# Products of zeros in spare PSUM banks, from the balancing to the first up matmuls

## The chip, the cores and the metric

The kernel runs on one core of one Trainium2 chip. The metric is the device time of one execution in microseconds (us); lower is better. A core has five engines that work side by side: PE (TensorE, matrix products), DVE (VectorE), ACT (ScalarE), POOL (GpSimd) and SP (SyncE, which here only issues transfers). Each takes its own instructions in order, and semaphores tie them together.

## The reference

Two parts follow each other. First an attention with sorted blocks: a small matrix of 8 x 8 per batch and head is balanced five times (rows and columns in turn), then it mixes the eight blocks of keys and values, and each block of queries attends to its mixed block. Then a feed-forward part with g = h cos(h).

```python
for _ in range(5):
    P = np.exp(P - np.max(P, axis=-1, keepdims=True))
    P = P / (np.sum(P, axis=-1, keepdims=True) + 1e-09)
    P = P / (np.sum(P, axis=-2, keepdims=True) + 1e-09)
k_sorted = np.einsum('bhij,bhjcd->bhicd', P, k_b)
v_sorted = np.einsum('bhij,bhjcd->bhicd', P, v_b)
scores = scale * np.matmul(q_b, k_sb.transpose(0, 1, 2, 4, 3))
attn = softmax(scores)
x = np.matmul(attn, v_sb)            # 3072 tokens x 512
h = x @ w_in                         # 512 -> 2048
out = (h * np.cos(h)) @ w_out        # 2048 -> 512
```

Batch 4, heads 8, sequence 768 (8 blocks of 96), head size 64.

## The kernel before, in words

The 3072 tokens are worked in eight chunks n of four blocks u each. For a chunk the stages are: scores (`qk`: products L422 or L427, row maximum L482 and subtraction L488 on DVE), exponent (`expo`, ACT, L506), transposition of the weights (`p_transpose`: eight transposes L532, and a copy to `pT`), weights times values (`av`, products L545, reciprocal L552 and scaling L554 on DVE), transposition of the result (`x_transpose`, L572, and a copy to `xT`), then `up` (products L585, cosine on ACT L589, product with h on DVE L592) and `down` (L609). The order of all of this is written out by hand from L674 on; no scheduler moves anything. Copies out of PSUM go through `copy_on`, so all of them on ACT have the line L288 and all on DVE L290.

Ahead of that stands the balancing (L266 to L352), for two groups g of two batches. Each of the four further rounds `it` has, per group, an exponent on ACT (L331), a product that sums (`product`, L262, tile `sk`) and three small steps on DVE (reciprocal L350, and L323 and L326 in `balance`). Between the rounds stand the transposes of the first queries (`q_products`, L301), whose results ACT copies to `q_turned` (twice, from two tiles `q_ps`). At the end of the last round DVE writes the balanced matrix spread out for the products, `bd` (L282).

Then come the sorted keys: `k_sort_0` makes products of key columns with `bd` (L360, tile `ks`) and copies them to `kTs` in four pieces. It is called for key columns 0 to 15 (copies on DVE), 32 to 39 (DVE), 16 to 31 (ACT) and 40 to 47 (ACT). `v_turn` (L436) makes `bdv`, and `v_sort_b` (L450, tile `vs`) makes eight columns of sorted values at a time and copies them to `vS` on ACT. The first calls of `qk` and the first up matmuls follow.

PSUM has eight banks here, in two pools. `acc` has two buffers of one bank, `big` three buffers of two banks (1024 float32 per partition). A tile in `big` always takes a buffer of two banks, also where it fills one or less: the tiles of `q_products`, `v_turn`, `p_transpose`, and those of `k_sort_0` and `v_sort_b` when they are told to use `big` (`*B` in the order; `*C` is `acc`).

`keep_warm(times)` (L216) takes a new tile `idle` in `big` and multiplies a matrix of zeros, `warm`, by one of its columns repeated 512 times, so many times (L220). Nothing reads the result. It is called with 17 ahead of the balancing, with 2 behind the first pair of `product`, and with 3 in the first further round.

Of the kernel before, what the change touches and what calls it, by code (L numbers as in the profile page):

```python
# [10 lines left out]
FP32 = mybir.dt.float32  # L11
BF16 = mybir.dt.bfloat16
# [6 lines left out]
def kernel(  # L19
# [15 lines left out]
    nc = tc.nc  # L35
    B, H, S, D = q.shape
    nb = sort_net.shape[-1]
    blk = S // nb
# [6 lines left out]
    H2 = H // 2  # L45
    NG = B // 2
    NN = 2 * H2 * nb
    IC = 4
# [5 lines left out]
    NB = H2 * nb  # L54

    const = ctx.enter_context(tc.tile_pool(name="const", bufs=1))
# [35 lines left out]
    def load(buf, r, src):  # L92
        nc.gpsimd.dma_start(out=buf[r:r + 64], in_=src)
# [7 lines left out]
    QR, NQ = 4, 3  # L101
# [101 lines left out]

    ones(0)
    order = const.tile([blk, blk], BF16, name="order")
    half_pi = const.tile([128, 1], FP32, name="half_pi")
    nc.vector.memset(half_pi[:], math.pi / 2)
    warm = const.tile([128, 128], BF16, name="warm")
    nc.vector.memset(warm[:], 0.0)
    nc.vector.memset(vperm[:, CD:], 0.0)  # L210
    nc.vector.memset(kbuf[:64, :32 * D], 0.0)

    early = const.tile([128, 1], FP32, name="early")
    nc.scalar.activation(early[:], half_pi[:], AF.Exp)

    def keep_warm(times):  # L216

        idle = big.tile([128, 512], FP32, name="idle", tag="big")
        for _ in range(times):
            nc.tensor.matmul(  # L220
                idle[:], warm[:], warm[:, :1].to_broadcast([128, 512]), start=True, stop=True)

    keep_warm(17)


# [34 lines left out]
    def product(lhs, rhs):  # L260
        ps = acc.tile([128, nb], FP32, name="sk", tag="acc")
        nc.tensor.matmul(  # L262
            ps[:], lhs.rearrange("p x j -> p (x j)"), rhs, start=True, stop=True)
        return ps

    for g in range(NG):  # L266
        nc.vector.reciprocal(ci[g][:], cs[g][:])
        nc.vector.scalar_tensor_tensor(
            L[g][:], rows_of, ci[g][:], along(E[g]), op0=ALU.mult, op1=ALU.mult)
    sk = [product(L[g], maskj[:]) for g in range(NG)]  # L270
    keep_warm(2)
# [22 lines left out]
    q_ps = {}  # L294

    def q_products(n, z, lo, hi, pool, tag):
        if lo == 0:
            q_ps[n, z] = pool.tile([128, 2, IC, QR, blk // QR], BF16, name="qps", tag=tag)
        for i in range(lo, hi):
            e, hp, r = i // (2 * QR), i // QR % 2, i % QR  # L300
            nc.tensor.transpose(  # L301
                q_ps[n, z][hp * D:(hp + 1) * D, e, :, r],
                q_rows[:, (z * 2 + e) * 2 + hp, r * D:(r + 1) * D], ident[:blk, :blk])
# [25 lines left out]
    for it in range(4):  # L329
        for g in range(NG):  # L330
            nc.scalar.activation(E[g], T[g], AF.Exp, scale=ci[g][:])  # L331
        if it == 3:
            copy_on(A, *turned[0])
        sk = [product(same, E[g]) for g in range(NG)]
        if it == 1:
            q_products(0, 0, 0, 12, big, "big")
        elif it == 2:
            turned = q_turn(0, 0, big, "big", 12)
            q_products(0, 1, 0, 8, big, "big")
        elif it == 3:  # L340
            turned = q_turn(0, 1, big, "big", 8)
            copy_on(A, *turned[0])
        keep_warm(3 if it == 0 else 0)
        if it == 1:

            nc.gpsimd.tensor_copy(held[:], cs[1][:])
            for z in range(3):
                load_w_in(z)
        for g in range(NG):
            nc.vector.reciprocal(rr[g], sk[g][:])  # L350
            if it < 3 or g == 0:
                balance(g)  # L352
# [4 lines left out]
    MH = H2 * IC  # L357
# [4 lines left out]

    def k_sort_0(t0, nt, eng, pool, tag):

        ps = pool.tile([128, nt, 2 * MH], FP32, name="ks", tag=tag)
        for t in range(nt):
            k_products(ps, t, t0 + t, slice(64, 128),
                       bds[0][64:, H:, :IC])
        ms, ts = slice(0, MH), slice(t0, t0 + nt)
        psv = ps.rearrange("p t (e m) -> p e m t", e=2)  # L370
        for hp in range(2):
            for x in range(2):
                copy_on(eng, kT[0][hp * D:(hp + 1) * D, hp + x, ms, ts],
                        psv[x * D:(x + 1) * D, hp])

    def k_cross(t0, nt, eng, pool, tag):

        ps = pool.tile([128, nt, 2 * MH], FP32, name="ks", tag=tag)
        for t in range(nt):
            k_products(ps, t, t0 + t, slice(64, 128), bds[0][64:, H:, IC:])  # L380
        ms, ts = slice(MH, 2 * MH), slice(t0, t0 + nt)
        copy_on(eng, kT[0][:, ::2, ms, ts], ps.rearrange("p t (e m) -> p e m t", e=2))
        nc.gpsimd.tensor_copy(kT[0][:D, 1, ms, ts], kT[0][D:, 0, ms, ts])
        nc.gpsimd.tensor_copy(kT[0][D:, 1, ms, ts], kT[0][:D, 2, ms, ts])

    def k_sort_1(t0, eng, pool, tag):
        ps = pool.tile([128, 8, 2 * NB], FP32, name="ks", tag=tag)
# [43 lines left out]
    bdv = const.tile([128, 2 * H, nb], BF16, name="bdv")  # L431

    def v_turn(eng=A):
        ps = big.tile([128, 128], FP32, name="bdp", tag="big")
# [7 lines left out]
        return vperm[:, d * blk:d * blk + 128] if permuted else vv[:, d]  # L442

    def v_sort_b(b, d0, nd, eng, pool, tag):
        ps = pool.tile([128, nd, 2 * NB], FP32, name="vs", tag=tag)


        rows, xs = slice(0, 64 + b * 64), slice((1 - b) * H, (2 - b) * H)
        for t in range(nd):
            nc.tensor.matmul(  # L450
                ps[:, t], v_cols(d0 + t, b == 1 or d0 + t >= D // 2)[rows],
                bdv[rows, xs].rearrange("p x i -> p (x i)"), start=True, stop=True)
# [48 lines left out]
    def expo(n, u, on_pe=False):  # L501
        p = p_bufs[cnt[0] % NP]
        cnt[0] += 1


        nc.scalar.activation(  # L506
            p[:, :, :blk], s_t.pop((n, u)).rearrange("p e h c -> p (e h) c"), AF.Exp,
            scale=scale)
# [18 lines left out]

    def p_transpose(n, u, eng, pool, tag):
        p = pb.pop((n, u))
        ps = pool.tile([128, 2 * H2, 128], BF16, name="pps", tag=tag)  # L530
# [147 lines left out]
    load_w_out(2)  # L678
    load_w_out(3)
    k_sort_0(0, 16, V, *C)  # L680
    v_turn()
    k_sort_0(32, 8, V, *B)
    k_sort_0(16, 16, A, *C)
    k_sort_0(40, 8, A, *C)
    v_sort_b(0, 0, 8, A, *C)
    qk(0, 0)
    qk(0, 1)
    v_sort_b(0, 8, 8, A, *B)
    v_sort_b(0, 16, 8, A, *C)
    expo(0, 0, True)  # L690
    v_sort_b(0, 24, 8, A, *C)
    load(kbuf, 0, kin_d[1])
    qk(0, 2)
    v_sort_b(0, 40, 8, A, *C)
    p_transpose(0, 0, A, *B)
    v_sort_b(0, 56, 8, A, *C)
    expo(0, 1, True)
    qk(0, 3)
    v_sort_b(0, 48, 8, A, *C)
    v_sort_b(0, 32, 8, A, *C)  # L700
    p_transpose(0, 1, A, *B)
# [12 lines left out]
    up(0, 0, 0, 2 * blk)  # L714
    p_transpose(0, 2, A, *C)
    up(0, 1, 0, 2 * blk)
# [227 lines left out]
```

## Time and profile before

| | us |
|---|---|
| three timed runs | 244.58, 245.59, 245.89; median 245.59 |
| the profiled execution | 245.65 |
| its span, first to last instruction | 243.9 |
| PE busy | 233.2 (96% of the span) |
| DVE busy | 173.8 (71%) |
| ACT busy | 157.6 (65%) |
| POOL busy | 88.0 (36%) |

The profile is one execution on the chip. A row of the timeline gives start and duration in us from the start of the span, the engine (PE are the products, PEld the loading of their fixed operand), the line of the kernel, the operation, the tile written and the tiles read, the shape, and how often. In brackets stands the engine's idle time before it and what ended it. The granted clock is the share of TensorE's full clock, 1.00 or 0.50 here. All products of zeros together have this row (busy time; mean ns of one):

```profile
L220 PE MATMUL idle<-warm 128*128 128x512 bf16 x22 | 7.0, 474 | 1.0 <-DVE warm L209 1.0
```

### The profile page before, as it was taken

What the parts mean: (1) busy time and instruction counts of PE and PEld (TensorE: products, weight loads), DVE (VectorE), ACT (ScalarE), POOL (GpSimd) and SP (SyncE); (2) the same over time, 40 slices, a digit from 0 to 9 for tenths busy, and PEclk for the clock granted to TensorE, in tenths of its full rate; (3) what the DMA queues carried; (4) which work ended last, traced back from release to release, by engine and by line L of the source; (5) the groups of instructions that cost most, each with busy time, mean ns of one, the idle gap of its engine ahead of it and who ended that gap; (6) DMA issues with size and microseconds to landing.
All of it is one profiled execution on the core that took longest, in us unless ns stands there. A gap on an engine that the chain in (4) does not pass through costs nothing.

```text
span 243.9 us, 5384 instructions
## 1 busy us (share of the span) xinstructions
PE 233.2 (96%) x2172; PEld 148.4 (61%) x2172; DVE 173.8 (71%) x320; ACT 157.6 (65%) x226; POOL 88.0 (36%) x110
## 2 busy tenths in 40 slices
PE   8879899899999999999999999999999999999994
PEld 3569698756576566655666656655565556456553
DVE  5568848996478965887668986898789768625700
ACT  3368866568288984888668956684567366737611
POOL 6359963599771099710443500800000000000000
PEclk9955569999999999999999999999999999999999
DMA  4999999991999961999898959924592660171012
GB/s 49 232 194 170 185 205 232 190 202 57 143 143 144 172 150 55 94 143 212 149 101 139 71 132 157 193 33 105 116 201 59 90 188 0 41 144 43 1 46 86
DMA packets 66681, 30.90 MB, mean 127 GB/s; under 512 B 55392, under 2 KB 62176, under 8 KB 66400
## 3 DMA queue, kind: packets, MB, share of 16 engines
q0 software_dynamic: 24048, 13.64, 41.9%
q1 hardware_dynamic: 42096, 16.72, 31.7%
q8 instruction: 17, 0.28, 0.5%
q10 hardware_dynamic: 512, 0.20, 0.3%
q14 instruction: 8, 0.07, 0.1%
HBM read 27.27 MB, written 6.29 MB: 138 GB/s over the span
## 4 chain that ended last, share of the span: by engine, by line
PE 79%; ACT 7%; DVE 6%; DMA 5%; issue 1%; DVEq 0%; ACTq 0%
PE h L585 33%; PE o L609 26%; PE sc L427 3%; PE av L545 3%; PE ks L360 3%; PE idle L220 2%; DMA vperm<-p_buf 2%; DMA xT<-xn 2%; ACT p_buf L506 2%; PE xps L572 2%; PE vs L460 2%; DVE gg L592 1%; PE vs L450 1%; ACT kTs L288 1%; ACT vS L288 1%
## 5 line engine op out<-in xcount | busy, mean ns | idle before, releaser
L585 PE MATMUL h<-xT,w_in_t 128*128 128x384 bf16 (+1 forms) x576 | 93.1, 313 | 0.5 <-DVE gg L592 0.2
L609 PE MATMUL o<-w_out_t,gg 128*128 128x512 bf16 x368 | 88.3, 379 | 0.5 <-DVE s L488 0.5
L589 ACT ACTIVATE c<-h,half_pi 128x768 f32<-128x768 f32 (+1 forms) x72 | 59.8, 830 | 29.2 <-PE h L585 27.0
L592 DVE TENSOR_TENSOR gg<-c,h 128x768 bf16<-128x768 f32 (+1 forms) x72 | 61.2, 860 | 23.0 <-ACT c L589 23.0
L585 PEld LDWEIGHTS <-w_in_t 128*128 128x128 bf16 x576 | 53.7, 100 | 27.8 <-issue 1.6
L609 PEld LDWEIGHTS <-gg 128*128 128x128 bf16 x368 | 33.2, 98 | 31.9 <-DVE s L488 0.7
L482 DVE TENSOR_REDUCE mx<-sc 96x4 f32<-96x384 f32 (+1 forms) x43 | 31.9, 743 | 2.9 <-PE sc L427 1.7
L488 DVE TENSOR_TENSOR s<-sc,mx 96x384 f32<-96x384 f32 (+1 forms) x43 | 32.2, 749 | 2.3
L177 POOL COPY vperm<-kv 64x1536 bf16<-64x1536 bf16 (+1 forms) x10 | 27.9, 2824 | 13.9 <-PE o L609 11.4
L506 ACT ACTIVATE p_buf<-s 96x768 bf16<-96x768 f32 x32 | 25.9, 839 | 1.1 <-DMA pT<-p_buf 0.7
L554 DVE TENSOR_TENSOR xn<-av,r 96x512 bf16<-96x512 f32 x32 | 22.0, 686 | 1.1
L427 PE MATMUL sc<-kTs,q_turned 128*128 128x96 bf16 x224 | 16.1, 206 | 0.7 <-DVE s L488 0.7
L134 POOL DMA_DIRECT2D kv<-in_q_dram x24 | 16.0, 674 | 0.7 <-issue 0.7
L552 DVE RECIPROCAL r<-av 96x8 f32<-96x8 f32 x32 | 6.4, 199 | 13.7 <-PE av L545 13.5
L427 PEld LDWEIGHTS <-q_turned 128*128 128x128 bf16 x224 | 12.9, 98 | 5.1 <-DVE s L488 1.3
L288 ACT COPY o_s<-o 128x512 f32<-128x512 f32 (+2 forms) x11 | 5.9, 538 | 14.9 <-PE o L609 8.6
L288 ACT CAST kTs<-ks 128x512 bf16<-128x512 f32 (+2 forms) x25 | 12.4, 497 | 4.8 <-PE ks L360 4.7
L288 ACT COPY kv<-o 128x512 f32<-128x512 f32 x8 | 4.7, 583 | 12.6 <-PE o L609 12.6
L134 POOL DMA_DIRECT2D q_mem<-in_q_dram x16 | 10.7, 677 | 0.3 <-issue 0.3
L589 ACT ACT_TABLE_LOAD x8 | 10.3, 1283 | 0.1
L288 ACT CAST pair<-vs 96x512 bf16<-96x512 f32 (+1 forms) x12 | 8.7, 728 | 2.0 <-PE vs L460 2.0
L288 ACT COPY xT<-xps 128x384 bf16<-128x384 bf16 (+1 forms) x9 | 4.6, 513 | 8.2 <-PE xps L572 8.2
(102 smaller groups left out, 225.4 us busy)
## 6 DMA issues: line engine op xcount, KB each, us to landing
out_dram<-kv SPq DMA_DIRECT2D x12, 256.0 KB, 2.8
out_dram<-o_s SPq DMA_DIRECT2D x11, 256.0 KB, 2.6
w_in_t<-in_moe_w_in_dram POOLq DMA_DIRECT2D x4, 512.0 KB, 9.2
w_out_t<-in_moe_w_out_dram POOLq DMA_DIRECT2D x4, 512.0 KB, 12.8
kv<-in_k_dram POOLq DMA_DIRECT2D x2, 768.0 KB, 13.4
kv<-in_v_dram POOLq DMA_DIRECT2D x2, 768.0 KB, 15.0
pair<-in_k_dram POOLq DMA_DIRECT2D x2, 768.0 KB, 11.1
kv<-in_v_dram POOLq DMA_DIRECT2D x6, 256.0 KB, 10.9
```

The costliest lines, as they stand in the source:

```text
L134: nc.gpsimd.dma_start(out=q_heads[:, i, :, e], in_=src[:, ih * IC + i, :, e])
L177: nc.gpsimd.tensor_copy(dst, src)
L288: eng.copy(dst, src)
L427: nc.tensor.matmul(out, q_of(n, hp)[:, x:x + 128], keys_of(n, u, h2, hp), start=True, stop=True)
L482: nc.vector.reduce_max(mx[:], scv, axis=AX.X)
L488: nc.vector.tensor_tensor(s, scv, mx.to_broadcast(list(s.shape)), op=ALU.subtract)
L506: nc.scalar.activation(p[:, :, :blk], s_t.pop((n, u)).rearrange("p e h c -> p (e h) c"), AF.Exp, scale=scale)
L554: nc.vector.tensor_tensor(xn.rearrange("p h e d -> p e h d"), avv[:, :, :, :D], r.to_broadcast([blk, 2, H2, D]), op=ALU.mult)
L585: nc.tensor.matmul(h[:, f2, :w], w_in_t[:, kk, f * 128:(f + 1) * 128], xT[n][:, kk, lo:hi], start=(kk == 0), stop=(kk == KC - 1))
L589: nc.scalar.activation(c[:, :, :w], h[:, :, :w], AF.Sin, bias=half_pi[:, 0:1])
L592: nc.vector.tensor_tensor(gt[n, fp][:, :, lo:hi], c[:, :, :w], h[:, :, :w], op=ALU.mult)
L609: nc.tensor.matmul(o[:], gt[n, f // 2][:, f % 2, ts * 128:(ts + 1) * 128], w_out_t[:, f, :], start=(f == 0), stop=(f == FC - 1))
```

## The change

`keep_warm` no longer takes a tile. A new function `bank` stands in for the allocation of most one-bank tiles: for the pool `big` it takes the whole two-bank tile, gives the caller the first bank, and remembers the second as `spare`; for `acc` it does what was done before. A call of `keep_warm` writes the spare bank of the tile that `bank` took last in `big`. The products of zeros grow from 22 to 59: between the two products of each round, two to four behind each round, and one to three at eighteen places of the order between the first keys and the first up matmuls. The `memset` of `warm` goes ahead of that of `half_pi`. Nothing else moves.

```diff
+    spare = [None]
+    def bank(pool, tag, shape, dtype, name):
+        if pool is not big:
+            return pool.tile(shape, dtype, name=name, tag=tag)
+        t = big.tile([128, 2, 512], FP32, name=name, tag=tag)
+        spare[0] = t[:, 1]
+        flat = t[:, 0] if dtype == FP32 else t[:, 0].bitcast(dtype)
...
-    def keep_warm(times):
-        idle = big.tile([128, 512], FP32, name="idle", tag="big")
+    def keep_warm(times, cols=512):
         for _ in range(times):
             nc.tensor.matmul(
-                idle[:], warm[:], warm[:, :1].to_broadcast([128, 512]), start=True, stop=True)
+                spare[0][:, :cols], warm[:], warm[:, :1].to_broadcast([128, cols]),
+                start=True, stop=True)
+    bank(big, "big", [128, 512], FP32, "idle")
     keep_warm(17)
...
-    sk = [product(L[g], maskj[:]) for g in range(NG)]
-    keep_warm(2)
+    for g in range(NG):
+        sk.append(product(L[g], maskj[:]))
+        keep_warm(1)
+    keep_warm(1)
...
-        sk = [product(same, E[g]) for g in range(NG)]
+        for g in range(NG):
+            sk.append(product(same, E[g]))
+            keep_warm(1 - g)
...
-        keep_warm(3 if it == 0 else 0)
+        keep_warm((4, 2, 2, 4)[it])
...
-        ps = pool.tile([128, nt, 2 * MH], FP32, name="ks", tag=tag)
+        ps = bank(pool, tag, [128, nt, 2 * MH], FP32, "ks")
...
     k_sort_0(0, 16, V, *C)
+    keep_warm(1)
     v_turn()
     k_sort_0(32, 8, V, *B)
+    keep_warm(1)
     k_sort_0(16, 16, A, *C)
+    keep_warm(3)
     k_sort_0(40, 8, A, *C)
+    keep_warm(2)
     v_sort_b(0, 0, 8, A, *C)
+    keep_warm(1)
     qk(0, 0)
     qk(0, 1)
     v_sort_b(0, 8, 8, A, *B)
+    keep_warm(1)
     v_sort_b(0, 16, 8, A, *C)
+    keep_warm(1)
     expo(0, 0, True)
     v_sort_b(0, 24, 8, A, *C)
+    keep_warm(1)
     load(kbuf, 0, kin_d[1])
     qk(0, 2)
     v_sort_b(0, 40, 8, A, *C)
     p_transpose(0, 0, A, *B)
+    keep_warm(1)
     v_sort_b(0, 56, 8, A, *C)
+    keep_warm(1)
     expo(0, 1, True)
     qk(0, 3)
     v_sort_b(0, 48, 8, A, *C)
+    keep_warm(1)
     v_sort_b(0, 32, 8, A, *C)
+    keep_warm(1)
     p_transpose(0, 1, A, *B)
+    keep_warm(2)
     expo(0, 2, True)
     av(0, 0, True)
     z_turned(1)
+    keep_warm(1)
     av(0, 1, True)
     expo(0, 3, True)
+    keep_warm(1)
     x_transpose(0, 0, V, *C)
+    keep_warm(2)
     x_transpose(0, 1, A, *C)
+    keep_warm(1)
...
     p_transpose(0, 3, V, *C)
+    keep_warm(1)
     up(0, 0, 0, 2 * blk)
```

The same replacement by `bank` stands in `q_products`, `k_cross`, `k_sort_1`, `v_turn`, `v_sort_b` and `p_transpose`.

More of the change, by code (lines that the diff above doesn't have):

```diff
@@ L205 @@
     order = const.tile([blk, blk], BF16, name="order")
+    warm = const.tile([128, 128], BF16, name="warm")
+    nc.vector.memset(warm[:], 0.0)
     half_pi = const.tile([128, 1], FP32, name="half_pi")
     nc.vector.memset(half_pi[:], math.pi / 2)
-    warm = const.tile([128, 128], BF16, name="warm")
-    nc.vector.memset(warm[:], 0.0)
     nc.vector.memset(vperm[:, CD:], 0.0)
@@ L214 @@
     nc.scalar.activation(early[:], half_pi[:], AF.Exp)
-    def keep_warm(times):
-        idle = big.tile([128, 512], FP32, name="idle", tag="big")
+    spare = [None]
[5 more added lines that the diff above has]
+        flat = t[:, 0] if dtype == FP32 else t[:, 0].bitcast(dtype)
+        names = "abcd"[:len(shape) - 1]
+        return flat[:, :math.prod(shape[1:])].rearrange(
+            f"p ({' '.join(names)}) -> p {' '.join(names)}",
+            **{c: w for c, w in zip(names, shape[1:])})
+    def keep_warm(times, cols=512):
         for _ in range(times):
             nc.tensor.matmul(
-                idle[:], warm[:], warm[:, :1].to_broadcast([128, 512]), start=True, stop=True)
+                spare[0][:, :cols], warm[:], warm[:, :1].to_broadcast([128, cols]),
+                start=True, stop=True)
+    bank(big, "big", [128, 512], FP32, "idle")
     keep_warm(17)
@@ L269 @@
             L[g][:], rows_of, ci[g][:], along(E[g]), op0=ALU.mult, op1=ALU.mult)
-    sk = [product(L[g], maskj[:]) for g in range(NG)]
-    keep_warm(2)
+    sk = []
+    for g in range(NG):
+        sk.append(product(L[g], maskj[:]))
+        keep_warm(1)
+    keep_warm(1)
     nc.vector.tensor_copy(same[:], rows_of)
@@ L297, in q_products @@
         if lo == 0:
-            q_ps[n, z] = pool.tile([128, 2, IC, QR, blk // QR], BF16, name="qps", tag=tag)
+            q_ps[n, z] = bank(
+                pool, tag, [128, 2, IC * QR * (blk // QR)], BF16, "qps").rearrange(
+                "p e (i r w) -> p e i r w", i=IC, r=QR)
         for i in range(lo, hi):
@@ L333 @@
             copy_on(A, *turned[0])
-        sk = [product(same, E[g]) for g in range(NG)]
+        sk = []
+        for g in range(NG):
+            sk.append(product(same, E[g]))
+            keep_warm(1 - g)
         if it == 1:
@@ L376, in k_cross @@
     def k_cross(t0, nt, eng, pool, tag):
-        ps = pool.tile([128, nt, 2 * MH], FP32, name="ks", tag=tag)
+        ps = bank(pool, tag, [128, nt, 2 * MH], FP32, "ks")
         for t in range(nt):
@@ L386, in k_sort_1 @@
     def k_sort_1(t0, eng, pool, tag):
-        ps = pool.tile([128, 8, 2 * NB], FP32, name="ks", tag=tag)
+        ps = bank(pool, tag, [128, 8, 2 * NB], FP32, "ks")
         for t in range(8):
@@ L433, in v_turn @@
     def v_turn(eng=A):
-        ps = big.tile([128, 128], FP32, name="bdp", tag="big")
+        ps = bank(big, "big", [128, 128], FP32, "bdp")
         for r in (0, 64):
@@ L444, in v_sort_b @@
     def v_sort_b(b, d0, nd, eng, pool, tag):
-        ps = pool.tile([128, nd, 2 * NB], FP32, name="vs", tag=tag)
+        ps = bank(pool, tag, [128, nd, 2 * NB], FP32, "vs")
         rows, xs = slice(0, 64 + b * 64), slice((1 - b) * H, (2 - b) * H)
@@ L529, in p_transpose @@
         p = pb.pop((n, u))
-        ps = pool.tile([128, 2 * H2, 128], BF16, name="pps", tag=tag)
+        ps = bank(pool, tag, [128, 2 * H2, 128], BF16, "pps")
         for a in range(2 * H2):
```

## The prediction

> **What bounds the kernel now.** I read the page first: the span, the clock row and the chain that ended last.
>
> ```profile
> span 243.9 us, 5384 instructions
> ...
> PEclk9955569999999999999999999999999999999999
> ...
> PE 79%; ACT 7%; DVE 6%; DMA 5%; issue 1%; DVEq 0%; ACTq 0%
> ```
>
> The chain is mostly PE, and the only slices with a low granted TensorE clock are the third to the sixth, about 12 to 36 us. The profiled execution took 245.65 us, 1.75 us more than its span; the median of the three timed runs, 245.59, is the same within 0.06, so I add to 245.65. Next the stretches around the low clock (columns: stretch, length, PE busy, granted clock, DMA share, GB/s).
>
> ```profile
> 8.01:11.42 3.41, 2.62 (x24) 1.00 1.01 213
> 11.42:14.84 3.42, 3.06 (x38) 0.50 0.97 189
> 14.84:18.25 3.41, 2.21 (x52) 0.50 1.26 212
> ...
> 28.49:31.90 3.41, 3.08 (x30) 0.50 1.35 200
> 31.90:35.32 3.42, 3.42 (x39) 0.50 1.24 205
> 35.32:38.73 3.41, 3.41 (x68) 1.00 1.29 229
> 45.56:48.97 3.41, 2.60 (x36) 1.00 1.26 204
> ```
>
> The clock is exactly half from 11.42 to 35.32, 23.9 us, seven times 3.41. PE "busy" does not tell why: 2.62 of 3.41 us came before the fall, and 2.60 of 3.41 at 45.56 keeps the full clock. What differs is how many columns streamed. Before the fall there were three products of zeros and twelve narrow transposes. The Trainium skill ("TensorE: Matmul & The Clock Gate", The HAM clock gate) says that activity is judged in free-running windows of 3413 ns; the trace agrees, with its 7 x 3.41.
>
> Is PE the limit inside this stretch? The timeline says who waits (columns: start, duration, engine, line, operation, tiles, shapes, count, idle time before):
>
> ```profile
> 13.62 0.54 PE L301 MATMUL qps<-ident,q_mem 96*64 96x96 bf16 x8
> ...
> 14.12 0.35 DVE L282 SCALAR_TENSOR_TENSOR bd<-maskp,ci,T 128x128 bf16<-128x128 f32 x1
> 14.22 0.80 ACT L288 COPY q_turned<-qps 128x768 bf16<-128x768 bf16 x1 [0.49 <-PE qps L301]
> 14.52 0.59 PE L360 MATMUL ks<-bd,kv 64*128 64x32 bf16 x16 [0.36 <-DVE bd L282]
> ...
> 15.15 2.97 DVE L290 CAST kTs<-ks 64x256 bf16<-64x256 f32 x8 [0.68 <-PE ks L360]
> ...
> 16.15 2.62 ACT L288 CAST kTs<-ks 64x256 bf16<-64x256 f32 x8 [0.48 <-PE ks L360]
> ...
> 18.81 0.80 PE L422 MATMUL sc<-kTs,q_turned 64*96 64x96 bf16 x15 [0.15 <-ACT kTs L288]
> ...
> 20.32 1.32 ACT L288 CAST vS<-vs 96x512 bf16<-96x512 f32 x2 [0.95 <-PE vs L450]
> ...
> 21.55 0.83 ACT L506 ACTIVATE p_buf<-s 96x768 bf16<-96x768 f32 x1
> ...
> 23.34 0.80 ACT L288 COPY pT<-pps 96x768 bf16<-96x768 bf16 x1
> ...
> 24.04 0.59 ACT L288 CAST vS<-vs 96x512 bf16<-96x512 f32 x1
> ```
>
> From 15 to 19 us the end of the stage is set by copies: DVE does eight and ACT does another eight beside them, and the first scores wait for ACT's. From 20.3 on ACT runs copy after copy without a gap. So up to there half clock costs little. It costs where the up matmuls begin:
>
> ```profile
> 26.33 0.80 ACT L288 COPY pT<-pps 96x768 bf16<-96x768 bf16 x1
> ...
> 28.11 0.69 DVE L554 TENSOR_TENSOR xn<-av,r 96x512 bf16<-96x512 f32 x1
> ...
> 29.40 0.48 ACT L288 COPY xT<-xps 128x384 bf16<-128x384 bf16 x1 [0.80 <-PE xps L572]
> ...
> 29.93 1.44 PE L585 MATMUL h<-xT,w_in_t 128*128 128x192 bf16 x8
> ...
> 36.15 0.83 PE L585 MATMUL h<-xT,w_in_t 128*128 128x192 bf16 x8
> ...
> 37.02 0.58 ACT L589 ACTIVATE c<-h,half_pi 128x384 f32<-128x384 f32 x1 [0.44 <-PE h L585]
> ```
>
> Eight up matmuls take 1.44 us at half clock, 0.83 at full.
>
> **The change part by part.** 37 products of 512 columns are added (59 for 22). Their price:
>
> ```profile
> 1.44 0.15 PEld L220 LDWEIGHTS <-warm 128*128 128x128 bf16 x1 [0.28 <-issue]
> 1.87 0.15 PEld L220 LDWEIGHTS <-warm 128*128 128x128 bf16 x1 [0.28 <-issue]
> ...
> 6.84 0.59 PE L220 MATMUL idle<-warm 128*128 128x512 bf16 x2
> ...
> 8.13 0.81 PE L220 MATMUL idle<-warm 128*128 128x512 bf16 x3
> ```
>
> Three minus two is 0.22 us each at full clock. The very first follow each other at 0.43, twice that (the clock row does not show it), which I take for half clock. PE takes its matmuls in order, so each product delays what stands behind it if PE is not idle there.
>
> The more important thing stands in the built program's waits. A spare bank is half of a tile whose other half a copy reads, and the dependency is kept by tile: a product of zeros that is issued after that copy waits for it. Five new waits come of this; the other edits (the swapped memsets, the reshaped tiles) leave ACT, DVE and POOL with the same instructions in the same order but for that swap. The waits, and behind each what is queued on PE:
>
> 1. Last round of balancing: four products wait for the second q_turned copy on ACT; behind them all key products (L360).
> 2. After the keys 32 to 39: one product waits for the last of DVE's eight kTs copies; behind it keys 16 to 31, which feed ACT's eight.
> 3. After v 8 to 15: one product waits for their vS copy; behind it v 16 to 23, ACT's next copy.
> 4. After the first p_transpose: one waits for the pT copy; behind it v 56 to 63, again ACT's next copy.
> 5. After the second p_transpose: two wait for the pT copy; behind them both av groups, ACT and DVE's way to xT.
>
> The sum, against the times of before, first at the half clock that I expect from 14.84 on (why: see rivals); "full" is the same sum at full clock.
>
> *Balancing.* Two products behind the transposes of the third round hold its successor's sk product by about 0.25; the full clock in the last round gives back 0.5. Net I take -0.27: bd starts at 13.85. Bounds: +1 if the clock falls at 11.42 as now, -0.5 if nothing is held.
>
> *Wait 1.* The transposes end at about 13.9, the copy (0.80) at 14.7. Four products: full 0.85, so L360 starts at 15.55 (+1.0 against 14.52); half from 14.84 on 1.58, so 16.28 (+1.75). bd, which ends it now, has long been there.
>
> *Wait 2.* From L360's start DVE's copies begin 0.63 later (15.15 less 14.52) and take 2.97. Half: 16.28 + 0.63 + 2.97 = 19.88, product 0.43, sixteen key products 0.59, handing over 0.05: ACT's copies begin at 20.95, not 16.15: +4.8. Full: 15.55 + 0.63 + 2.97 + 0.22 + 0.59 + 0.05 = 20.0: +3.85. What ran side by side now runs one after the other; this is the largest term. Behind it, at half clock, three products, eight keys, two products, v 0 to 7 and one product (6 x 0.43 + 0.3 + 0.65) end at about 24.15, later than ACT's copies (20.95 + 2.66 = 23.6): scores at 24.15, not 18.81: +5.35. Full: ACT's copies stay last, +3.85.
>
> *Wait 3.* ACT's two vS copies at 20.32 no longer join: between them stand a product and eight v products, half 0.43 + 0.85 + 0.05 = 1.35. A row for those eight:
>
> ```profile
> 17.70 0.85 PE L450 MATMUL vs<-bdv,kv 64*128 64x64 bf16 x8 [0.38 <-ACT kTs L288]
> ```
>
> So +6.7. At full clock I take about half of it, 0.7, less 0.3 that scores and v products come sooner: +4.3.
>
> *Wait 4.* The same with v products from vperm: half 0.43 + 0.62 + 0.1 = 1.2, +7.9; full 0.7, +5.0. Row:
>
> ```profile
> 21.86 0.62 PE L450 MATMUL vs<-bdv,vperm 64*128 64x64 bf16 x8
> ```
>
> *To the second pT copy.* At half clock PE has three more products on the way (1.3) and becomes later than ACT by about 1.0: +9.0, the copy ends at 36.1 where it ended at 27.13. Full: +5.3.
>
> *Wait 5.* From that copy to the end of xT took 29.88 - 27.13 = 2.75. Now two products, av, one product, av, then reciprocal and xn twice (0.2 + 0.69), four transposes and two products. Half until the next border of 3.41 us at 38.73: 4.35, so +10.6. Full: 3.9, so +6.5.
>
> *Up matmuls.* With the clock at full by then, the ACT table load, the cosines and three groups at 0.83 instead of 1.44 win back about 0.85 by the cosine of 37.02. Half case: +9.8; full: +5.65.
>
> Does it carry to the end? In the chain from 36 to 167 us every piece is PE, ACT or DVE; no transfer ends a wait there, and transfers that are already queued only land earlier relative to their use. I let it carry whole: 245.65 + 9.8 = **255.4 us**. If DVE and POOL collide less, up to 0.5 may come back.
>
> **The rivals.**
>
> *Clock at full throughout, waits as above: 251.3* (245.65 + 5.65). For: the products add up to 1.7 us of streaming in 8.01 to 11.42, about half of that window. Against: 11.42 to 14.84 would hold only about 0.85 us of products, plus transposes; then PE stands for some 2.7 us behind wait 2. The window that lost the clock held this now:
>
> ```profile
> 8.01:11.42 3.41, 0.81 (x3) 1.00 1.01 213
> ```
>
> If transposes do not count, that is the same load, and the clock falls at 14.84. The Trainium skill (same page, Part 4) says that transposes do not count in the same way; by that the forecast stands. Its section "Why this matters for your kernels" asks only that no PE gap exceed about 3 us; by that rule the clock would stay full and the time be this rival's, 251.3. The trace speaks against it: all idle time of PE in 8.01 to 11.42 is 3.41 - 2.62 = 0.79, and the clock fell.
>
> *Clock falls at 11.42 all the same: 257.* The last round and wait 1 then come about 1.6 later than in the forecast.
>
> *Faster: 244.2.* The clock stays full and the five waits end early: then the up matmuls give 0.85, the balancing 0.27, the shorter way from pT to xT some 0.3. It decides at wait 2: only if DVE's copies were over before PE asks could this be, and they begin after the keys and take 2.97. Very unlikely. That nothing changes (245.6) would need the gain and wait 2 to cancel.
>
> *Part of the delay is absorbed* later, by a transfer that is late now: about 249 to 250. I see none in the chain.
>
> **How the numbers follow.** Forecast (half clock for most of the stage, own range 253.5 to 256.5) 0.62; fall at 11.42 0.12; full clock 0.17; absorbed 0.03; faster 0.04; same 0.02. The range from 251.0 to 257.6 leaves out little over 1 in 10. Half a per cent, 1.2 us, is about what a measurement of this kernel can tell from no change. Slower: 0.62 + 0.12 + 0.17 + 0.03 = 0.94; same 0.02; faster 0.04.
>
> **What would show it.** Wait 2: the L360 products that feed ACT's kTs copies start after the end of DVE's eight, and ACT's copies at 20 us or later. Wait 1: the first L360 product over 1 us after bd. Waits 3 and 4: idle ACT of 0.7 to 1.3 before a vS copy that follows a vS or pT copy. Clock: a fall at 14.84 or 18.25 (an 11.42 or none gives the rivals), a rise near 38.73 or 42.15. The cosine that stood at 37.02 stands near 46.8. It would be wrong if ACT's kTs copies still began by 17 us, or if the later stages shrank by more than 1 us.

## The result, and the profile after

The changed kernel takes **260.18 us** (median of four runs, 259.97 to 260.70) against 245.09 for the kernel before beside it (four runs, 244.55 to 245.89): a ratio of 1.0616, 95% interval 1.0576 to 1.0656. It is slower, as forecast, but by 15.1 us where 9.8 were forecast, and outside the range of 251.0 to 257.6. Executions over 1.5% longer than the fastest of the same kernel in the same session are left out of every median, range and ratio from here on.

The profiled execution took 259.97 us. Three lines of its page, to be held against those of before: span, clock in 40 slices, and the chain that ended last by engine.

```profile
span 258.2 us, 5431 instructions
...
PEclk9997555999999999999999999999999999999999
...
PE 80%; DVE 7%; ACT 5%; DMA 5%; issue 2%; SPq 0%; ACTq 0%; DVEq 0%
```

The low digits of the clock row, 5556 in the third to sixth slice before, are 7555 in the fourth to seventh: the products moved the low clock and did not end it. The stretches by the clock's own borders show it exactly (columns: stretch, length, busy time of PE, PEld, DVE, ACT, POOL, then granted clock, DMA share, GB/s).

```profile
13.44:16.86 3.42, 2.51 (x31) 1.55 (x30) 1.11 (x7) 1.78 (x3) 1.62 (x2) 1.00 1.01 164
16.86:20.27 3.41, 0.93 (x22) 0.72 (x19) 2.84 (x8) 0.27 (x1) 3.41 (x2) 1.00 1.24 208
20.27:23.69 3.42, 3.42 (x30) 1.21 (x29) 0.00 (x0) 2.19 (x7) 3.42 (x5) 0.50 0.99 137
23.69:27.10 3.41, 2.73 (x35) 2.14 (x34) 1.71 (x2) 1.49 (x4) 1.57 (x3) 1.00 1.16 176
27.10:44.17 17.07, 14.13 (x126) 9.79 (x129) 8.86 (x17) 9.54 (x14) 9.62 (x11) 0.50 1.22 213
```

Half clock for 3.42 + 17.07 = 20.5 us, where it was 23.9 before, and later. In 16.86 to 20.27, the window ahead of the first fall, DVE worked (2.84) and PE stood (0.93). The products of zeros alone in the first four of these windows (columns: window, length, busy time and number on PE and on PEld, then as above):

```profile
13.44:16.86 3.42, 1.66 (x7) 0.57 (x5) 1.00 1.01 164
16.86:20.27 3.41, 0.13 (x1) 0.19 (x2) 1.00 1.24 208
20.27:23.69 3.42, 2.69 (x6) 0.42 (x5) 0.50 0.99 137
23.69:27.10 3.41, 0.77 (x3) 0.19 (x2) 1.00 1.16 176
```

The clock of a window goes with the window ahead of it: behind seven of these products comes full clock, behind one half, behind six full again, behind three half. So the idle window kept the full clock, and the next one paid. The timeline of after says behind what PE stood, and then who stood behind PE:

```profile
14.74 0.35 DVE L300 SCALAR_TENSOR_TENSOR bd<-maskp,ci,T 128x128 bf16<-128x128 f32 x1
...
15.59 1.03 PE L233 MATMUL qps<-warm 128*128 128x512 bf16 x4 [0.91 <-ACT q_turned L306]
...
16.56 0.56 PE L383 MATMUL ks<-bd,kv 64*128 64x32 bf16 x16
...
17.16 2.93 DVE L308 CAST kTs<-ks 64x256 bf16<-64x256 f32 x8 [2.06 <-PE ks L383]
...
20.14 0.49 PE L233 MATMUL ks<-warm 128*128 128x512 bf16 x1 [2.23 <-DVE kTs L308]
...
21.21 1.50 ACT L306 CAST kTs<-ks 64x256 bf16<-64x256 f32 x4 [3.29 <-PE ks L383]
...
26.87 0.39 PE L233 MATMUL vs<-warm 128*128 128x512 bf16 x1 [0.68 <-ACT vS L306]
...
28.14 0.59 ACT L306 CAST vS<-vs 96x512 bf16<-96x512 f32 x1 [1.32 <-PE vs L473]
...
30.99 0.59 ACT L306 CAST vS<-vs 96x512 bf16<-96x512 f32 x1 [0.86 <-PE vs L473]
...
31.79 0.80 ACT L306 COPY pT<-pps 96x768 bf16<-96x768 bf16 x1 [0.21 <-PE pps L555]
...
32.64 0.58 PE L233 MATMUL pps<-warm 128*128 128x512 bf16 x1 [0.88 <-ACT pT L306]
...
33.80 0.58 ACT L306 CAST vS<-vs 96x512 bf16<-96x512 f32 x1 [1.21 <-PE vs L473]
...
37.51 0.80 ACT L306 COPY pT<-pps 96x768 bf16<-96x768 bf16 x1 [0.59 <-PE pps L555]
...
38.36 1.01 PE L233 MATMUL pps<-warm 128*128 128x512 bf16 x2 [0.88 <-ACT pT L306]
...
42.69 0.48 ACT L306 COPY xT<-xps 128x384 bf16<-128x384 bf16 x1 [2.90 <-PE xps L595]
...
49.28 0.58 ACT L612 ACTIVATE c<-h,half_pi 128x384 f32<-128x384 f32 x1 [0.44 <-DVE r L575]
```

All five forecast waits are there: every L233 row in this fence has a copy as its releaser (q_turned, kTs, vS, pT, pT), and behind each the next copy comes late. The clearest pair: DVE's eight kTs copies end at 17.16 + 2.93 = 20.09, the product of zeros follows at 20.14, and ACT's kTs copies, which ran beside DVE's before (16.15), begin at 21.21, +5.06. The cosine of 37.02 stands at 49.28: +12.27.

From there the delay holds to 88 us. Then it grows once more, by 2.1, to +14.37 at the cosine of 198.08. Of that, 1.35 comes at one place. First the kernel before (SPq is SP's queue, which issues transfers), then after:

```profile
87.22 1.28 SPq L519 DMA_TRANSPOSE pT<-p_buf  x1
...
89.99 0.68 PE L545 MATMUL av<-vS,pT 96*128 96x65 bf16 x16
```

```profile
99.54 1.26 SPq L542 DMA_TRANSPOSE pT<-p_buf  x1
...
103.64 0.69 PE L568 MATMUL av<-vS,pT 96*128 96x65 bf16 x16 [1.17 <-DMA pT<-p_buf]
```

The same transfer is issued in both, and in after PE waits 1.17 us for it. The DMA view of the time from issue to landing, before and then after (packets, MB, share; then us to landing):

```profile
q1 hardware_dynamic: 1095, 0.49, 67.8%
...
pT<-p_buf SPq DMA_TRANSPOSE x1, 2.6
```

```profile
q1 hardware_dynamic: 1266, 0.53, 47.6%
q8 instruction: 1, 0.02, 1.4%
...
pT<-p_buf SPq DMA_TRANSPOSE x1, 4.1
```

It took 4.1 us instead of 2.6, and one packet of queue q8, a piece of the program itself, was fetched meanwhile. In before no such piece falls into this transfer. Nearly all of the rest, 0.9, comes between the cosines of 124 and of 150. The pT transfer that was issued there at 142.7 in before landed in 2.6 us; in after it took 4.15, again with a piece of q8 in it, and PE waits for it:

```profile
160.78 0.39 PE L568 MATMUL av<-pair,pT 96*128 96x65 bf16 x7 [0.70 <-DMA pT<-p_buf]
```

### The profile page after: what moved, and what is told of

The parts are those of the page before. It is cut to its first block, busy times and chain, and to the rows that moved or that the text cites. A ratio compares the mean times of both kernels' runs of the same rounds, so it can differ in the third digit from the quotient of the medians.

```text
span 258.2 us, 5431 instructions
## 1 busy us (share of the span) xinstructions
PE 240.9 (93%) x2183; PEld 149.2 (58%) x2209; DVE 173.8 (67%) x320; ACT 157.9 (61%) x226; POOL 87.7 (34%) x110
## 4 chain that ended last, share of the span: by engine, by line
PE 80%; DVE 7%; ACT 5%; DMA 5%; issue 2%; SPq 0%; ACTq 0%; DVEq 0%
PE h L608 30%; PE o L632 24%; PE av L568 3%; DMA pT<-p_buf 3%; PE idle L233 3%; PE sc L450 3%; PE vs L473 3%; PE ks L383 2%; DVE gg L615 2%; PE pps L233 2%; PE xps L595 2%; PE pps L555 1%; DVE s L511 1%; PE vs L483 1%; DVE mx L505 1%
## 5 line engine op out<-in xcount | busy, mean ns | idle before, releaser
L608 PE MATMUL h<-xT,w_in_t 128*128 128x384 bf16 (+1 forms) x576 | 91.4, 309 | 0.5 <-issue 0.2
L632 PE MATMUL o<-w_out_t,gg 128*128 128x512 bf16 x347 | 84.9, 379 | 1.6 <-DVE s L511 0.5
L608 PEld LDWEIGHTS <-w_in_t 128*128 128x128 bf16 x576 | 52.5, 98 | 27.5 <-issue 1.2
L306 ACT CAST vS<-vs 96x512 bf16<-96x512 f32 x16 | 9.2, 583 | 5.7 <-PE vs L473 5.5
L233 PEld LDWEIGHTS <-warm 128*128 128x128 bf16 x59 | 7.0, 129 | 8.3 <-issue 5.8
L568 PEld LDWEIGHTS <-pT 96*128 96x128 bf16 (+1 forms) x160 | 7.5, 105 | 6.3 <-DMA pT<-p_buf 2.5
## 6 DMA issues: line engine op xcount, KB each, us to landing
kv<-in_v_dram POOLq DMA_DIRECT2D x6, 256.0 KB, 10.6
```

Source lines behind the costliest of these rows:

```text
L233: nc.tensor.matmul(spare[0][:, :cols], warm[:], warm[:, :1].to_broadcast([128, cols]), start=True, stop=True)
L306: eng.copy(dst, src)
L608: nc.tensor.matmul(h[:, f2, :w], w_in_t[:, kk, f * 128:(f + 1) * 128], xT[n][:, kk, lo:hi], start=(kk == 0), stop=(kk == KC - 1))
L632: nc.tensor.matmul(o[:], gt[n, f // 2][:, f % 2, ts * 128:(ts + 1) * 128], w_out_t[:, f, :], start=(f == 0), stop=(f == FC - 1))
```

## The experiments

Theory: the loss is (a) the five waits, (b) the products' own streaming in PE's way, most of it at half clock, and (c) something in the later stages. Rivals: that (a) is small and streaming or the clock is the cause; that the new allocation costs by itself; for (c), that a late start of the later stages costs, or the products themselves, rather than where the program's pieces are fetched. No kernel here changes what is computed: the products of zeros are read by nothing.

The table gives for each kernel the median (or the one time where there is one run), and how much later than in the kernel before three instructions start in its profile: ACT's kTs copies (16.15 before), the cosine of 37.02, and the cosine of 198.08; each is one start from a timeline less another. The last column is the time to landing of the transfer shown above, and whether a piece of q8 lies in it.

| kernel | us | kTs copy | cosine 37 | cosine 198 | pT landing |
|---|---|---|---|---|---|
| before | 245.09 to 245.43 | 0 | 0 | 0 | 2.6, none |
| after | 260.18 | +5.06 | +12.27 | +14.37 | 4.1, piece |
| 1 older banks, no waits | 252.03 | +0.50 | +3.73 | +6.08 | 4.1, piece |
| 2 waits, narrow products | 254.40 | +3.80 | +6.21 | +8.73 | 4.1, piece |
| 3 after without wait 2 | 254.95 | +1.30 | +6.68 | +9.32 | 4.4, piece |
| 4 new allocation alone | 245.32 | +0.53 | -0.27 | -0.34 | 2.6, none |
| 5 before, more instructions first | 249.24 | +1.27 | +0.19 | +3.52 | 4.2, piece |
| 6 as 1, narrow (second run) | 249.54 | +0.50 | +1.24 | +3.52 | 4.2, piece |
| 7 as 1, balancing only | 246.02 | -0.19 | -0.21 | +0.11 | 2.6, none |
| 8 as 1, 256 more instructions (second run) | 250.93 | +3.60 | +6.09 | +6.08 | 2.6, none |
| 9 as 1, wait 2 put back | 256.47 | +3.39 | +8.49 | +11.12 | 4.4, piece |

**1. All products, but without a wait.** Each product that waited writes to the spare bank of an older tile, whose copy is long over; one call moves ahead of a `v_sort_b`.

```diff
-    def keep_warm(times, cols=512):
+    def keep_warm(times, cols=512, at=None):
+        at = spare[0] if at is None else at
...
-        keep_warm((4, 2, 2, 4)[it])
+        keep_warm((4, 2, 2, 4)[it], at=at_idle if it == 3 else None)
...
+    at_k = spare[0]
-    keep_warm(1)
+    keep_warm(1, at=at_q)
...
-    keep_warm(2)
+    keep_warm(2, at=at_p)
```

> All 59 products of zeros stay, at the same places but one, and write the spare bank of an older tile whose copy is long over (the one behind v 8 to 15 moves ahead of these products). So the five waits for copies in flight are gone. Waits theory: the 14 us go away nearly whole; what is left is some 0.2 to 0.4 per product that stands in PE's way, less up to 1.5 if the clock holds: 243.5 to 247, ACT's kTs copies begin by 17 us. Rival, PE's time: 37 products at 0.22 to 0.43 are 8 to 16 us by themselves and stay: 253 to 260.

Measured: 252.03 us (251.40 to 254.06, six runs), ratio 1.0288 [1.0258, 1.0318]. The waits, with what they did to the clock, are worth 260.18 - 252.03 = **8.15 us**, over half of the loss. Neither expectation came out: the time lies between 243.5 to 247 and 253 to 260, so the products cost much by themselves too, if less than the rival said. Its timeline behind the first keys:

```profile
16.05 0.56 PE L386 MATMUL ks<-bd,kv 64*128 64x32 bf16 x16
16.54 0.82 PE L235 MATMUL qps<-warm 128*128 128x512 bf16 x3
16.64 2.62 ACT L309 CAST kTs<-ks 64x256 bf16<-64x256 f32 x8 [0.84 <-PE ks L386]
```

ACT's copies run beside DVE's again. Its stretches:

```profile
17.90:21.31 3.41, 3.35 (x41) 2.64 (x40) 1.67 (x3) 2.10 (x7) 3.41 (x3) 1.00 1.24 206
21.31:34.96 13.65, 13.53 (x118) 8.41 (x117) 8.59 (x16) 8.82 (x14) 13.40 (x17) 0.50 1.19 179
```

The clock falls all the same, at 21.31, and from there to 34.96 PE is busy for 13.53 of 13.65 us: with the waits gone it is the bound, at half clock, and the products are in its way. Note what the window before the fall says of gaps: PE was busy in 3.35 of its 3.41 us. Only four products of zeros were among it, where the window ahead, which was followed by full clock, had eight. The Trainium skill ("TensorE: Matmul & The Clock Gate", Why this matters for your kernels) asks that PE not be idle for more than about 3 us; no gap there came near that, and the clock fell. The row decides: a PE without gaps is not enough.

**2. The waits without the streaming.** In the changed kernel, the products from the second further round on get 8 columns instead of 512.

```diff
-    keep_warm(1)
+    keep_warm(1, 8)
```

(at every call; the first 17 and the first round keep 512)

> The changed kernel, with 8 columns instead of 512 in every product of zeros from the second further round on (the 17 first, the 3 behind the first pair and the 5 of the first round stay). The waits stay, the products' own time is nearly gone, and the clock must fall about as in the kernel before. Waits theory: the eight kTs copies of ACT still come behind DVE's, and the three later waits still cost a handing over each: 251 to 254. Rival, PE's time or a delay by the products' streaming: back to 245 to 247.

Measured: 254.40 us (one run), just above the 251 to 254 expected. The product of zeros costs nothing now and still waits:

```profile
19.20 0.17 PE L233 MATMUL ks<-warm 128*128 128x8 bf16 x1 [2.33 <-DVE kTs L308]
...
19.95 2.62 ACT L306 CAST kTs<-ks 64x256 bf16<-64x256 f32 x8 [3.10 <-PE ks L383]
```

So half of the delay at the cosine of 37.02 needs no streaming at all: +6.21 of +12.27, against +1.24 for the same narrow products without waits (experiment 6).

**3. Wait 2 alone taken away.** In the changed kernel the product behind keys 32 to 39 and the six behind it go to an older bank; the four other waits stay.

```diff
+    at_q = spare[0]
...
     k_sort_0(32, 8, V, *B)
-    keep_warm(1)
+    keep_warm(1, at=at_q)
```

> The changed kernel, with the one product behind keys 32 to 39 and the six after it written to the spare bank of the older q tile, so that wait 2 (for DVE's eight kTs copies) alone is gone; the other four stay. Waits theory: DVE's and ACT's copies run side by side again, 2.9 to 3.5 us come back: 256.5 to 257.3, and ACT's kTs copies begin near 18 us. Rival, PE's time: 259.5 to 260.5. If the clock alone made the loss, the clock rows tell, and 260.

Measured: 254.95 us (one run): wait 2 is worth 5.2 us here, more than the 2.9 to 3.5 expected. ACT's copies:

```profile
17.45 2.62 ACT L308 CAST kTs<-ks 64x256 bf16<-64x256 f32 x8 [0.84 <-PE ks L385]
```

In this execution the balancing also began 1.3 earlier than in that of after (-0.35 against +0.97 at the exponent of 7.26), so experiment 9 asks the same from the other side.

**4. The allocation alone.** `bank` and all reshaped tiles stay; the products are 17, 2 and 3 as before.

> The new allocation alone: one-bank tiles take the first bank of a two-bank tile, products of zeros go to the spare bank, in the counts and at the places of the kernel before (17, 2 and 3). Both theories: same as before, 245 to 246, with the same half clock from about 11.4 to 35.3. A cost here would mean that the allocation or the swapped memsets cost something by themselves.

Measured: 245.32 us (nine runs, 244.31 to 246.12), ratio 0.9997 [0.9982, 1.0012], nothing lost later. The allocation is free.

**5. More PE instructions in the kernel before.** 15 full and 39 narrow first products instead of 17: 37 more products, 74 more PE instructions with their weight loads, none of them behind a wait.

```diff
-    keep_warm(17)
+    keep_warm(15, 39)
```

> The kernel before, with 15 full and 39 narrow (8 columns) products of zeros first, not 17 full ones: 37 more pairs of weight load and product on PE, as many as the change adds, but ahead of everything, with no new wait. In the trace of the changed kernel a 16 KB piece on the instruction queue lies on the transfer of pT near 101 us, which landed 1.4 us late; in the kernel before that piece comes at another place. Theory that the mere number of PE instructions moves these pieces: the stretch from the eighth cosine group's place (37.02 us before) to the end grows from 206.9 to about 208.9 us, total 246 to 249. Rival (the later start changes how transfers meet): 206.9, total 244.5 to 246.5.

Measured: 249.24 us (248.36 to 251.72, four runs), ratio 1.0154 [1.0082, 1.0225]; the profiled execution took 249.16. Up to the up matmuls hardly anything is lost (+0.19), and then 3.3 us are, more than the 2.0 expected; 2.2 of them (+0.40 to +2.64) between the cosines of 85 and of 97, where PE waits for the same transfer:

```profile
88.42 1.27 SPq L522 DMA_TRANSPOSE pT<-p_buf  x1
...
92.62 0.55 PE L548 MATMUL av<-vS,pT 96*128 96x65 bf16 x12 [1.83 <-DMA pT<-p_buf]
```

```profile
q8 instruction: 1, 0.02, 1.3%
...
pT<-p_buf SPq DMA_TRANSPOSE x1, 4.2
```

The stage is only 0.40 late there and no product of zeros is near: the late loss comes with the further instructions alone, and the rival of a late start falls. Not all of it is the piece: in this profile the transfer is also issued 1.20 later than before (88.42 for 87.22), 0.8 more than the stage is late; it lands another 1.6 late.

**6. No waits and next to no streaming.** Experiment 1 with 8 columns, in two runs.

```diff
-    keep_warm(3, at=at_q)
+    keep_warm(3, 8, at=at_q)
```

(and so at every call from the second further round on)

> The run with other spare banks (no wait for a copy in flight), and 8 columns instead of 512 in the products of zeros from the second further round on. Neither the waits nor the products' streaming are left, only 37 more pairs of instructions. If waits and streaming are the whole cost of the first 50 us: 245 to 246 there, plus the 2 us later on: 246.5 to 248. If the later 2 us come of the shifted start: 245 to 246.

> The same kernel as the one with narrow products in older banks, whose profile was disturbed: no waits, next to no streaming, all 37 further products. If waits and streaming are all that the products cost ahead of the up matmuls, the cosine of 35.07 stands within 1.1 us of its place, as it did there, and what is lost after that is the 3 us that further PE instructions alone cost (249.2 in the profiled execution of the kernel before with them): 248 to 249.5 us. If the extra 3.9 us between 35 and 88 us of that profile belong to the kernel, it comes out at 252 or more again.

Measured: first 249.33 us (248.32 to 250.40, three runs; ratio 1.0121 [1.0031, 1.0211]), then 249.54 (248.93 to 252.14, four runs; ratio 1.0214 [1.0140, 1.0288] against its own runs of before). Both lie above the 246.5 to 248 of the first expectation. The profile of the first is of an execution of 253.11 us; its 3.9 us between 35 and 88 us did not come again, and the table has the second. That one is +1.24 at the cosine of 37.02 and +3.52 at the end, the same +3.52 as experiment 5. So 37 products that neither wait nor stream for long cost 1.2 ahead and 2.3 behind.

**7. The products of the balancing alone.** Experiment 1 with no product behind the balancing.

```diff
-    keep_warm(1, at=at_idle)
...
-    keep_warm(2, at=at_p)
```

(and so all calls from the first keys on)

> The run with other spare banks, without any product of zeros behind the balancing: 14 more than before, no wait for a copy in flight. The clock should hold until 14 to 18 us and the last round be faster by 0.3 to 0.6: 244.5 to 245.5. If products hold the rounds up, or the 28 more instructions matter later: 245.5 to 247.

Measured: 246.02 us (244.99 to 248.20, eleven runs), ratio 1.0042 [1.0007, 1.0076], as the second expectation had it. The full clock does help the last round, but the gain is gone at once:

```profile
13.62 0.35 DVE L303 SCALAR_TENSOR_TENSOR bd<-maskp,ci,T 128x128 bf16<-128x128 f32 x1
...
14.49 0.56 PE L386 MATMUL ks<-bd,kv 64*128 64x32 bf16 x16
```

`bd` comes 0.5 earlier than 14.12, but four products stand ahead of the keys, which begin at 14.49 where they began at 14.52. What it loses, it loses later: -0.22 at the cosine of 97 becomes +0.48 at that of 124. Its 28 further PE instructions move a piece of q8 into another pT transfer, issued at 115.8, which takes 4.09 us; in before the same one, at 116.3, has no piece in it and takes 2.68.

**8. A whole piece more.** Experiment 1 with 12 full and 96 narrow first products instead of 17: with the 37 further on, 128 products and their 128 weight loads more than before (2300 loads to 2172), 256 PE instructions. The page gives 0.28 MB for 17 pieces, about 16 KB each. The experiment assumes that 256 PE instructions fill one such piece, so that every later instruction lies in its piece where it lay before; the page's count of pieces will say.

```diff
-    keep_warm(17)
+    keep_warm(12)
+    keep_warm(96, 8)
```

> The run with other spare banks, with 12 full and 96 narrow products first, not 17 full ones: with the 37 pairs of the change 128 pairs, 256 instructions of 64 bytes, so one piece of 16 KB, more than before. If the place of the instruction pieces makes the later loss, it goes away: from the place of 37.02 to the end about 207 us, not 208.9, whatever the start does (250 to 252 in all). Rival: 208.5 to 209.

> The same kernel as the one with 256 further PE instructions, with times: 12 full and 96 narrow first products, the rest as in the kernel with products in older banks. If the place of the instruction pieces costs the 2 us in the later stages, it takes 251 to 251.6 although its up matmuls begin some 2 us later than in the kernel with 17 full ones (252.03): from the cosine of 35.07 to the end it takes some 2.5 us less than that one. If the late loss comes from the products themselves, it takes 254 or more.

Measured: 251.33 us in one run, then 250.93 (248.56 to 251.71, three runs), ratio 1.0217 [1.0143, 1.0291]. The page shows one piece more, as assumed, and the timeline and the DMA view of the second run no wait:

```profile
q8 instruction: 18, 0.29, 0.5%
```

```profile
93.36 1.27 SPq L546 DMA_TRANSPOSE pT<-p_buf  x1
...
96.12 0.68 PE L572 MATMUL av<-vS,pT 96*128 96x65 bf16 x16
```

```profile
pT<-p_buf SPq DMA_TRANSPOSE x1, 2.6
```

The up matmuls begin 2.4 later than in experiment 1 (+6.09 against +3.73), for the 96 products stand ahead of the balancing, and yet the end is the same (+6.08 both): nothing is lost behind the cosine of 37.02, with the same products in the same places. The rival that the products themselves cost later falls too.

**9. Wait 2 alone put back** into experiment 1.

```diff
     at_k = spare[0]
-    keep_warm(1, at=at_q)
+    keep_warm(1)
```

> Wait 2 is put back alone into the kernel with products in older banks (252.03 us): the one product behind the keys 32 to 39 writes again to the bank beside the one that DVE's eight kTs copies read; no other product waits for a copy in flight. If the waits' costs simply add, wait 2 is worth what its removal alone brought, 254.95 against 260.2, some 4 to 5 us: 256 to 257 us, ACT's kTs copies 4 us later than in the kernel without waits (about 20.5, not 16.64), and the first cosine of the up matmuls as much later. The rival: what wait 2 costs is partly hidden behind what PE has to do anyway with the other products, so that alone it is worth under 3 us, 253 to 255.

Measured: 256.47 us (256.01 to 257.58, four runs), ratio 1.0470 [1.0425, 1.0515]. One product of 0.38 us costs 256.47 - 252.03 = **4.4 us** (5.0 between the two profiled executions, 256.72 and 251.72):

```profile
18.60 0.38 PE L235 MATMUL ks<-warm 128*128 128x512 bf16 x1 [2.24 <-DVE kTs L311]
...
19.54 1.50 ACT L309 CAST kTs<-ks 64x256 bf16<-64x256 f32 x4 [3.16 <-PE ks L386]
```

ACT's copies come 2.9 later than in experiment 1 (16.64), not the 4 expected, and the cosine of 37.02 4.76 later. Between the two the clock has its part: it was half for 20.5 us here (19.07 to 39.55), for 13.65 in experiment 1. So wait 2, with the clock that it brings, is worth 4.4 with the others gone and 5.2 (one run) with the others there, of 8.15 for all five.

**The account.** In the profiles, +14.37 at the cosine of 198.08 is 3.52 for further instructions that neither wait nor stream (experiment 6; 2.3 of it behind the cosine of 37.02), 6.08 - 3.52 = 2.56 for their streaming (1 less 6), and 14.37 - 6.08 = 8.29 for the waits (after less 1). Each share includes what it did to the clock, which was half for 20.5 us in after, 13.65 in experiment 1 and 23.9 in experiment 6; no run separates the two. No version with more products beat the kernel before; the nearest, experiment 7, does not gain.

## Why the prediction was right and where it failed

*Waits 1 to 5: right in mechanism, near in size, and in part by luck.* Wait 1 moved the keys by 2.04, from 14.52 to 16.56; forecast +1.0 (full clock) to +1.75. The clock was full there, so +1.0 is the figure to compare, and 0.97 of the 2.04 was a late start (next paragraph). Wait 2 moved ACT's copies by 5.06; forecast +4.8 at half clock, +3.85 at full. That it came near the first is luck: the clock was full up to 20.27, and the late start made up for it. Taken from the first keys on, the way to ACT's copies grew from 16.15 - 14.52 = 1.63 to 21.21 - 16.56 = 4.65, by 3.0; the forecast at full clock was 2.8. ACT's idle time before the copies behind waits 3 and 4 is 1.32 and 1.21; forecast 1.35 and 1.2. The way from the second pT copy to the end of xT took 43.17 - 38.31 = 4.86; forecast 4.35. That wait 2 is the largest term is shown by experiments 3 and 9. One sum has a slip: the terms given for the scores at 24.15 add up to 24.43; they stand at 24.94.

*Balancing: right once the start is taken off.* `bd` is at 14.74, +0.62, not -0.27. But the exponent of 7.26 already stood +0.97: the first 17 products ended later, because the clock rose at 6.62, not at 4.60. From there to `bd` the change gains 0.35. The prediction gave the start of the clock's windows no bound; in experiments 1 and 3, with the same first products, that exponent stood at -0.19 and -0.35. On its own this is not lost to the end: in experiment 4 it stood at +0.94 and the cosine of 37.02 at -0.27.

*The clock: its borders right but for their start.* Forecast were a fall at 14.84 or 18.25 and a rise near 38.73 or 42.15; it fell at 20.27, came back for one window, fell at 27.10 and rose at 44.17. In multiples of 3.41 from the first rise at 6.62 these are the 4th, 5th, 6th and 11th border; counted from 4.60, the 4th and the 11th are the prediction's 18.25 and 42.15. It was half for 20.5 us of the stage, where the forecast's borders give 23.9: the window in which it came back was not forecast. The rivals with the clock full throughout, and with a fall at 11.42, were both wrong.

*The step that failed first: between wait 3 (+6.7) and wait 4 (+7.9) the sum has nothing but wait 4, and only behind it says "PE has three more products on the way (1.3) and becomes later than ACT by about 1.0", +9.0.* In after the copies behind these two waits are at +7.1 (28.14, for 21.05, the second of the two at 20.32) and at +9.76 (33.80, for 24.04): 2.7 apart, not 1.2. Half of that, 1.35, is there by the first pT copy (31.79 for 23.34, +8.45), ahead of wait 4. PE was late before that wait: the copy at 30.99 waits 0.86 for it and the pT copy 0.21, neither of which had idle time before, and two of the products of zeros, behind v 16 to 23 and v 24 to 31, stand in PE's way there. So the second pT copy is at +11.18, not +9.0, xT at +13.29, not +10.6, and the cosine at +12.27, not +9.8. Experiment 1 says what was overlooked: without any wait PE is the bound from 21.31 to 34.96, so that each product there counts in full and not only where a wait stands. The prediction priced the products mainly as queues behind five waits and put those between waits 3 and 4 at nothing.

*The step that failed second: "I let it carry whole."* It carried whole to 88 us and then grew by 2.1. The prediction had looked for transfers that were late; the transfer that became late was neither issued later in its stage nor larger, but shared its time with a piece of the program. In the table, all seven profiles with such a piece in it show 4.1 to 4.4 us, and all four without one 2.6. The two later pT transfers, issued at 113.0 and 142.7 in before, show the same: 4.06 to 4.41 us in those seven profiles, with a piece that starts 1.8 to 2.4 us after the issue, and 2.6 to 2.8 in the other four. Experiments 5 and 8 make this more than a coincidence: 74 more PE instructions bring the loss into the kernel before, 256 take it out of the kernel with products.

The two misses, 2.5 and 2.1, make up the 4.6 us between +9.8 and +14.37.

*The other rivals.* "Faster" failed where the prediction said it would be decided: DVE's copies ended at 20.09, after PE had asked for 2.23 us. "Absorbed" went the other way.

*Left open.* What exactly the clock counts isn't settled. In all profiles of these runs, a window with full clock ahead of the up matmuls was followed by full clock where six or more products of zeros of 512 columns ran in it, and by half where four or fewer did; five went both ways. How much narrower products and transposes count, and what brings a half clock back, is open: in after six in a half-clock window did (20.27 to 23.69), in experiment 9 five did not (19.07 to 22.48). The waits 1, 3, 4 and 5 were not taken away one by one. Why a piece of about 16 KB makes a transfer land some 1.5 us later is not shown, only that it does. The late loss in after is 1.35 by the cosine of 97, 0.18 more by that of 124, 0.89 more by that of 150, each behind one of the three transfers with a piece in it. The 0.37 that comes back by 198 comes back in experiments 4 and 7 too, so it is not of the products.

## What to carry to other kernels

A filler instruction is only free if nothing that it touches is in use: on an engine that takes its instructions in order, one product of 0.38 us that waits for a copy in the other half of its tile cost 4.4 us; two engines that had copied side by side did so in turn, and the clock was half for longer. Before filling idle time on an engine, ask whether the same stretch will still have idle time once the filler is in; here PE became the bound at half clock. And when code grows ahead of a stage, look whether the later stages have changed in the profile though nothing in them was edited.

## What the runs showed of the hardware that was not expected

- Instructions are fetched in pieces of about 16 KB over the DMA engines. A piece that started 1.4 to 2.4 us after the issue of a transposing transfer of pT made it land after 4.1 to 4.4 us; the same transfers without a piece landed after 2.6 to 2.8 (q8 in the DMA view). 74 further PE instructions, which by themselves cost 0.2 us, so cost 3.3 us; 256 further ones moved the pieces by one and cost nothing there.
- The clock's windows of 3.41 us start at another time in each execution: with the same first 17 products, the first rise lay at 3.91 in experiment 3 and at 6.62 in after, and with it the end of the first products and every later border.
- A busy PE did not hold the full clock, and an idle one did not lose it at once: in experiment 1 the clock fell behind a window with 3.35 of 3.41 us busy, in which four products of zeros of 512 columns ran; in after it stayed full through a window with 0.93 of 3.41 busy, behind one with seven such products, and fell at its end.
